# The last block's partial sums in another buffer, and the order of issue read from a table

## The chip, the cores and the metric

The kernel is written in Bass with Tile for a Trainium2 chip and runs on one of its cores. A core has five engines that run side by side, each through its own list of instructions in order: TensorE (PE: matrix products into PSUM), VectorE (DVE) and ScalarE (ACT: elementwise work), GpSimd (POOL) and SyncE (SP), which here issues every DMA. Where one engine needs what another makes, its instruction waits for a semaphore, and everything behind it in that engine's list waits with it.

The metric is the device time of one execution in microseconds, the median of several runs.

## The reference

q, k, v and g_ln are float32, the weight matrices 64-bit floats. The reference runs three stages, and each feeds the next:

```
B, H, S, D = 4, 8, 576, 64
scores = q @ k.T / sqrt(D)                       # per batch and head
mask   = local (rel in 0..31)  for heads 0..3,  strided (pos % 32 equal, rel >= 0)  for heads 4..7
x      = softmax(mask(scores)) @ v               # x: 2304 tokens x 512
h      = x @ w_in                                # 512 -> 1024
solu   = h * softmax(h);  ln = (solu - mean) / sqrt(var + 1e-6) * g_ln
y      = ln @ w_out                              # 1024 -> 512
out    = ((y @ w_a) * (y @ w_b)) @ w_out2        # 512 -> 1536 -> 512
```

The kernel reads each weight as a pair of 32-bit words and converts it itself.

## The kernel before

**Stages.** The attention runs batch by batch; scores, softmax and the product with V are made in tiles of a pair of heads. The strided heads use one form of mask, the local heads another. For batch 0's strided and local heads the probabilities are transposed on TensorE (L820) and multiplied with V in float32 (L854). For the other batches they are split into a high and a low half in float16 (`P2`), transposed by a DMA (`dma_start_transpose`, L842), and multiplied in three passes (L859 to L861), after a scale for V has been found by a chain of small steps (`pow2_scale`: TensorE L555, VectorE, TensorE L560, VectorE, TensorE L570). ScalarE copies the result to `xT` (L881). Tokens that are done go through the first feed-forward stage in tiles of 128 (`moe1`): x is split in two halves, L912 makes 1024 columns in three passes of 4 matmuls for each half, VectorE, ScalarE and GpSimd make softmax and normalisation, a DMA transposes the result, and `s2` multiplies by `w_out` (L966) and stores y to DRAM. All 2304 tokens pass before the last stage begins.

The last stage works on three blocks of 768 tokens (`SB`, `NSB`) and, for each, in three passes over thirds of the 1536 columns (`NP`, `UP`): nine blocks `b0` in all. The products of a block (L1392) follow a scheme with seven in place of eight products, for which y is split into sums and halves (`y_load`, L1306 to L1360). For passes 1 and 2 the last product (`out_pair`) follows the same scheme: seven products of six matmuls each per pair of token tiles, in two PSUM banks called M and N (L1530), with results updated by VectorE (L1546). For pass 0 it is `out_tile` (L1499).

**Partial sums.** A pass ends with 256 KB per token tile. Passes 0 and 1 store it to `o_scr` in DRAM; passes 1 and 2 load what the pass before has stored into a tile `ob` (L1517), add to it in place (L1546), and store it: to `o_scr` again, or to the output (L1568; in the very last pair column half by column half, L1573). There are two `ob` buffers of 128 x 2 x 512 numbers, used in turn, one for a pair. A block has three pairs.

**Weights.** Each 512 KB of raw weights comes in by `from_f64`: a DMA into one of three `raw64` buffers (L506, L509), a conversion on ScalarE (L510), a shift on VectorE (L516) and a merge on VectorE (L520). For `w_in`, ScalarE then rounds to a first half (L529) and GpSimd makes the rest (L530). `early` converts part of the last stage's weights during the attention and stores them to `w_scr` in DRAM, from where `conv_ab` reads them. A tile `yst` (128 x 4 x 768 float32) first holds y blocks while `y_load` splits them, and later the raw output weights of a pass (`conv_o`, `split_o`).

**What sets the order.** The program does not issue instructions as it goes. `P.op` notes an operation with its engine, its cost in the planner's eyes, what it reads and writes, and a function that emits it; operations are numbered as they are noted (3132 of them, 0 to 3131). At the end `Plan.schedule` puts them in one list, and `emit` calls them in that order, so that each engine gets its own operations in the order of the list. A dependency between engines becomes a semaphore wait. In the kernel before, `schedule` first follows due times (`P.key`), and then makes 200 further attempts: a backward pass gives each operation a key, noise is added, a forward pass lays the operations out with the planner's costs, and the order with the shortest result is kept.

Of the kernel before, what the change touches and what calls it, by code (L numbers as in the profile page):

```python
# [61 lines left out]


# [34 lines left out]
class Plan:  # L98

    TICK, ENTRY, SWITCH = 10.24 / 3, 2710, 0.095
    SAME = dict(DVE=0.13, ACT=0.15, POOL=0.05, PE=0.0, CTL=0.0)
    ENGINES = ("ACT", "CTL", "DVE", "PE", "POOL", "SP")

# [37 lines left out]
    def latency(self, a, b):  # L143
        if a.eng == b.eng and a.eng != "SP":
            return self.SAME[a.eng]
        return 0.28 if a.eng == "PE" else 0.14

    def schedule(self):


        ops, n = self.ops, len(self.ops)
        self.eng = [self.ENGINES.index(o.eng) for o in ops]
        self.us, self.cols, self.mode = [o.us for o in ops], [o.nbytes for o in ops], [o.mode for o in ops]
        self.deps = [[(d.seq, self.latency(d, o)) for d in sorted(o.deps, key=lambda d: d.seq)] for o in ops]
        self.starts = [[d.seq for d in sorted(o.starts, key=lambda d: d.seq)] for o in ops]
        self.outs, self.souts = [[] for _ in ops], [[] for _ in ops]
        for i in range(n):
            for d, lat in self.deps[i]:
                self.outs[d].append((i, lat))
            for d in self.starts[i]:  # L160
                self.souts[d].append(i)
        key, shift = [o.key for o in ops], 0.0
        order = self.forward(key, shift)
        self.mean = self.length(order)
        best = order, key, shift
        rnd = random.Random(PARAM["seed"])
        for t in range(PARAM["passes"]):
            if t % PARAM["back"] == 0 and t >= PARAM["first"]:
                self.forward(best[1], best[2])
            key = [k + rnd.gauss(0.0, PARAM["noise"]) for k in self.backward()]  # L170
            shift = self.TICK * (t % 4) / 4
            order = self.forward(key, shift)
            length = self.length(order)
            if length < self.mean:
                self.mean, best = length, (order, key, shift)
        return [ops[i] for i in best[0]]

    def length(self, order):
        return sum(self.replay(order, self.TICK * (k + 0.5) / 3) for k in range(3)) / 3

    def matmuls(self, count, t, us, cols):

        tick, per = self.TICK, cols / us if us else 0.0
        while True:
            w = int(t / tick)
            rate = 1.0 if w and count[w - 1] >= self.ENTRY else 0.5
            room = (w + 1) * tick - t
            if us <= room * rate:
                count[w] += per * us
                return t + us / rate  # L190
            count[w] += per * room * rate
            us -= room * rate
            t = (w + 1) * tick + 1e-9

    def replay(self, order, shift):
        eng, us, cols, deps, starts, mode, PE, SP = self.eng, self.us, self.cols, self.deps, self.starts, self.mode, 3, 5
        free, start, end = [0.0] * 6, [0.0] * len(eng), [0.0] * len(eng)
        count, dma, hw, was = [0.0] * 1000, 0.0, 0.0, 0
        for i in order:
            e = eng[i]  # L200
            at = free[e]
            for d, lat in deps[i]:
                x = end[d] + lat
                if x > at:
                    at = x
            for d in starts[i]:
                if start[d] > at:
                    at = start[d]
            start[i] = at
            if e == PE:  # L210
                x = us[i] if mode[i] == was else us[i] + self.SWITCH
                was = mode[i]
                end[i] = free[e] = self.matmuls(count, at + shift, x, cols[i]) - shift
            elif e == SP:
                hw = max(hw, at) + 0.55
                dma = max(dma, hw + 0.65) + cols[i] / 250e3
                free[e] = max(at + us[i], hw, dma - 2.0)
                end[i] = dma + 0.75
            else:
                end[i] = free[e] = at + us[i]  # L220
        return max(end)

    def forward(self, key, shift):
        eng, us, cols, outs, souts, mode, PE, SP = self.eng, self.us, self.cols, self.outs, self.souts, self.mode, 3, 5
        n = len(eng)
        left = [len(self.deps[i]) + len(self.starts[i]) for i in range(n)]
        ready, start, end = [0.0] * n, [0.0] * n, [0.0] * n
        free, coming, able = [0.0] * 6, [[] for _ in range(6)], [[] for _ in range(7)]
        push, pop = heapq.heappush, heapq.heappop
        for i in range(n):  # L230
            if not left[i]:
                push(coming[eng[i]], (0.0, i))
# [1451 lines left out]
```

## Time and profile before

| what | us |
|---|---|
| median of 3 runs | 705.09 |
| lowest and highest run | 704.83 and 705.89 |
| the profiled execution's own time | 706.01 |
| its span, first to last instruction | 704.2 |
| TensorE busy (95% of the span) | 671.1 |
| VectorE busy (79%) | 557.6 |
| ScalarE busy (61%) | 429.2 |
| GpSimd busy (21%) | 145.2 |
| mean granted clock of TensorE | 0.975 |

The profile is of one execution, which took 0.9 us more than the median. An engine is busy while it executes; waiting, branching and issuing DMAs don't count. Lines (L1530) are those of the kernel before. A row of the order of time gives start, duration, engine, line, operation and, in brackets, how long the engine had stood idle before and what ended that. `x3` means that three such instructions are drawn together. Matmuls overlap, since they are pipelined; their ends are modelled. The granted clock is a share of full speed: 1.00 is 2.4 GHz, 0.50 is 1.2 GHz.

### The profile page before, as it was taken

How to read it: one execution, taken by the hardware profiler on the slowest of the kernel's cores; microseconds unless marked ns; L12 is line 12 of the kernel's file. 1: busy time of each engine (PE TensorE's matmuls, PEld its weight loads, DVE VectorE, ACT ScalarE, POOL GpSimd, SP SyncE). 2: the span in 40 equal slices, each digit the busy share in tenths (PEclk: the TensorE clock that was granted, in tenths of full speed). 3: DMA queues.
4: the chain of work that ended last, by engine and by line, in shares of the span. 5: the costliest groups of instructions: out<-in, count | busy, mean ns of one | idle time of the engine just before them, and what ended most of it. 6: DMA issues, size and time to landing. Idle time of an engine off the chain costs nothing.

```text
span 704.2 us, 15205 instructions
## 1 busy us (share of the span) xinstructions
PE 671.1 (95%) x5861; PEld 483.9 (69%) x5861; DVE 557.6 (79%) x1189; ACT 429.2 (61%) x842; POOL 145.2 (21%) x268
## 2 busy tenths in 40 slices
PE   6877889999999999999899999999999999999996
PEld 5655668887888888886555555556767676776675
DVE  5878978967989654998999947779898978886584
ACT  3759757676877754867767537676545635534430
POOL 4544525633675442410000000000000000000000
PEclk9968789999999999999999999999999999999998
DMA  8978979889999834766462041672435206441035
GB/s 181 244 216 210 158 193 204 192 179 233 217 211 251 227 82 97 202 202 219 137 226 86 16 165 37 201 233 83 130 106 180 91 1 190 147 135 46 1 121 180
DMA packets 152645, 109.68 MB, mean 156 GB/s; under 512 B 103670, under 2 KB 128764, under 8 KB 152572
## 3 DMA queue, kind: packets, MB, share of 16 engines
q1 hardware_dynamic: 152572, 108.71, 58.5%
q8 instruction: 46, 0.75, 0.4%
q14 instruction: 27, 0.22, 0.1%
HBM read 65.42 MB, written 27.53 MB: 132 GB/s over the span
## 4 chain that ended last, share of the span: by engine, by line
PE 85%; DVE 5%; DMA 4%; ACT 2%; issue 1%; SPq 1%; POOL 0%; DVEq 0%; POOLq 0%; ACTq 0%
PE N L1392 19%; PE M L1392 14%; PE h L912 13%; PE y L966 13%; PE M L1499 6%; PE N L1530 6%; PE M L1530 5%; PE s L664 2%; DMA raw<-in_moe_w_a_dram 1%; PE s L757 1%; PE xbank L859 1%; DMA raw<-in_moe_w_b_dram 1%; DMA rawq<-in_q_dram 1%; DMA raw<-in_moe_w_in_dram 1%; DVE f64f L520 1%
## 5 line engine op out<-in xcount | busy, mean ns | idle before, releaser
L1392 PEld LDWEIGHTS <-w 128*128 128x128 f16 x1512 | 147.9, 98 | 95.3 <-issue 1.3
L1392 PE MATMUL N<-y,w 128*128 128x384 f16 x864 | 155.5, 326 | 0.0
L1392 PE MATMUL M<-y,w 128*128 128x384 f16 x648 | 119.2, 326 | 0.9 <-DVE y L1335 0.9
L966 PE MATMUL y<-lnT,wout 128*128 128x256 f16 x864 | 102.8, 275 | 2.1 <-ACT wout L579 2.1
L966 PEld LDWEIGHTS <-wout 128*128 128x128 f16 x864 | 82.5, 98 | 15.3 <-ACT wout L579 2.4
L912 PE MATMUL h<-win,xh 128*128 128x512 f32 x288 | 80.7, 423 | 2.4 <-DVE wk L927 2.4
L1530 PEld LDWEIGHTS <-p 128*128 128x128 f16 x693 | 67.7, 98 | 15.6 <-issue 3.5
L912 PEld LDWEIGHTS h<-win,xh 128*128 128x128 f32 x288 | 55.8, 201 | 14.5 <-DVE wk L927 2.6
L1484 ACT CAST p<-A 128x384 f16<-128x384 f32 x101 | 50.5, 512 | 22.1 <-DVE A L1459 19.6
L1489 DVE TENSOR_TENSOR p<-A,p 128x384 f16<-128x384 f32 x101 | 54.6, 552 | 6.6 <-ACT p L1484 6.4
L1530 PE MATMUL N<-wo,p 128*128 128x256 f16 x396 | 51.4, 273 | 3.1 <-DVE ob L1546 3.1
L1499 PE MATMUL M<-wo,p 128*128 128x512 f16 x216 | 49.9, 379 | 1.0 <-DVE A L1459 0.6
L510 ACT ACTIVATE f64f<-raw 128x512 f32<-128x512 f32 x52 | 34.6, 671 | 13.2 <-DMA raw<-in_moe_w_a_dram 4.9
L912 PE MATMUL h<-win,xl 128*128 128x512 f32 x144 | 40.1, 401 | 0.0
L1530 PE MATMUL M<-wo,p 128*128 128x256 f16 x297 | 38.6, 273 | 0.0
L1499 PEld LDWEIGHTS <-p 128*128 128x128 f16 x216 | 21.1, 98 | 24.6 <-issue 1.5
L833 POOL TENSOR_TENSOR e<-e,r 128x324 f32<-128x324 f32 (+2 forms) x30 | 27.2, 913 | 46.9 <-DVE r L794 43.2
L917 DVE TENSOR_REDUCE st<-h 128x1 f32<-128x1024 f32 x18 | 22.0, 1220 | 17.6 <-PE h L912 17.4
L1546 DVE SCALAR_TENSOR_TENSOR ob<-N,osc,ob 128x256 f32<-128x256 f32 x54 | 24.3, 477 | 14.3 <-PE N L1530 10.1
L1399 ACT COPY N<-N 128x384 f32<-128x384 f32 x36 | 16.6, 465 | 30.1 <-PE N L1392 29.5
L912 PEld LDWEIGHTS h<-win,xl 128*128 128x128 f32 x144 | 27.4, 194 | 6.4 <-issue 0.2
L841 POOL TENSOR_TENSOR P<-e,P 128x324 f16<-128x324 f32 (+2 forms) x30 | 28.4, 954 | 11.3 <-ACT P L840 11.2
(194 smaller groups left out, 1242.1 us busy)
## 6 DMA issues: line engine op xcount, KB each, us to landing
raw<-in_moe_w_out_dram SPq DMA_DIRECT2D x20, 512.0 KB
o_scr<-ob SPq DMA_DIRECT2D x36, 256.0 KB
ob<-o_scr SPq DMA_DIRECT2D x36, 256.0 KB
raw<-in_moe_w_a_dram SPq DMA_DIRECT2D x12, 512.0 KB
raw<-in_moe_w_b_dram SPq DMA_DIRECT2D x12, 512.0 KB
y_scr<-y SPq DMA_DIRECT2D x14, 384.0 KB
y<-y_scr SPq DMA_DIRECT2D x14, 384.0 KB
y_scr<-ys SPq DMA_DIRECT2D x18, 256.0 KB
```

What stands on the lines that cost most here:

```text
L510: act(0.67, lambda: nc.scalar.activation(f(), raw()[:, :, 1].bitcast(F32), AF.Prelu, scale=2.0 ** -112, alpha=-2.0 ** 32), (raw,), (f,))
L833: pool(0.1 + 1.2 * pl, lambda: nc.gpsimd.tensor_tensor(ev(), ev(), r()[:, :ng].unsqueeze(2).to_broadcast([128, ng, nk]), op=ALU.mult), (r, ...
L841: pool(0.15 + 1.4 * pl, lambda: nc.gpsimd.tensor_tensor(plo, ev(), ph, op=ALU.subtract), (e, ("P2", pi, 0)), (("P2", pi, 1),))
L912: nc.tensor.matmul(h()[:, 512 * n:512 * n + 512], xs[xa]()[:, kk], win[wa][:, kk, 512 * n:512 * n + 512], start=(pi == 0 and kk == 0), sto ...
L917: dve(1.22, lambda: nc.vector.tensor_reduce(st()[:, 0:1], h(), axis=AX.X, op=ALU.max, negate=True), (h,), ((st, 0),))
L966: nc.tensor.matmul(y()[:, 256 * mi:256 * mi + 256], wout[:, kk, wa, 128 * m:128 * m + 128], lnT()[:, xa, kk], start=(pi == 0 and kk == 0), ...
L1392: nc.tensor.matmul(to()[:, :HB], w()[:, wa, a, kk], y7[b]()[:, xa, kk], start=first and pi == 0 and kk == 0, stop=pi == 2 and kk == 1, ski ...
L1484: act(0.5, lambda: nc.scalar.copy(pu(0, a), x()), (x,), (pu.tok(0, a),))
L1489: dve(TD, lambda: nc.vector.tensor_tensor(pu(1, a), x(), pu(0, a), op=ALU.subtract), (x, pu.tok(0, a)), (pu.tok(1, a),))
L1499: nc.tensor.matmul(o(), pus[u](xa, 2 * t + c)[:, 128 * w:128 * w + 128], wo_whole(ps, 2 * u + c)[:, wa], start=(u == 0 and c == 0 and pi = ...
L1530: nc.tensor.matmul(bk(i), pus[u](xa, a)[:, 128 * tt:128 * tt + 128], wo()[:, u, b, wa], start=a == A11 and u == 0 and pi == 0, stop=u == U ...
L1546: dve(0.475, lambda: nc.vector.scalar_tensor_tensor(dst(), bk(i), s(), dst(), op0=ALU.mult, op1=ALU.add), (src, osc), ((ob, t, c),))
```

## The change

There are two parts.

First, in the last of the nine blocks `out_block` takes one more turn of the tile `yst` and hands it to `out_pair` as `spare`. The three pairs then use three separate parts of it (3 x 1024 of its 3072 columns), and no `ob`. Loads, updates and stores are as many and as large as before.

Second, the planner's passes are gone, and `schedule` returns the operations in the order of a list of their numbers, `ISSUE`. The operations and their numbers are the same as before. What an operation emits is unchanged, except for the buffer above. The numbers that the text below speaks of, with their place among their engine's operations in the order of before and in the table:

| number | what | engine, line | place before | in the table |
|---|---|---|---|---|
| 181 | load of the first block of `w_in` | SP L509 | 15 | 6 |
| 182 | its conversion | ACT L510 | 7 | 3 |
| 183, 184 | its shift and its merge | DVE L516, L520 | 28, 30 | 18, 25 |
| 190 | the merge of the second block | DVE L520 | 40 | 39 |
| 830, 853, 865 | products with V of batch 2's strided heads | PE L859 to L861 | 175, 180, 184 | 153, 157, 171 |
| 790, 792, 795 | a scale chain | PE L555, L560, L570 | 118, 145, 151 | 167, 170, 175 |
| 1084 | conversion of a block of `w_b` | ACT L510 | 191 | 199 |
| 1703 | first split of y for the second block | DVE L1335 | 484 | 479 |
| 1601, 1604, 1636 | halves of the first block's products | DVE L1489 | 470, 472, 478 | 493, 494, 497 |
| 1630, 1633 | sums of the first block's products | DVE L1403 | 480, 482 | 485, 487 |
| 1777 | an output product of the first block | PE L1499 | 401 | 403 |
| 3073, 3074, 3092, 3093, 3111, 3112 | loads of the last block's partial sums | SP L1517 | 384, 383, 389 to 392 | 365 to 370 |
| 3104 | last product of the last pair but one | PE L1530 | 792 | 790 |
| 3119, 3120 | products of the last pair | PE L1530 | 789, 791 | 791, 792 |
| 3123 | its last product | PE L1530 | 793 | 793 |

Of TensorE's 793 operations 292 keep their place, and the largest move is 49 places; of VectorE's 1024 it is 243, of ScalarE's 760 201, of GpSimd's 154 77, of SyncE's 398 138.

The diff, with the table and the passes taken out cut to a few lines:

```diff
+ISSUE = [int(n) for n in """
+5 0 13 2 14 1 11 15 10 12 29 6 16 8 35 181 9 4 3 37 7 36 414 430 771 787 39 38 43 40 41 182 66 44 17 55 42 45 67 56 20
+46 183 68 70 57 47 58 71 69 48 59 49 60 50 184 74 18 19 61 185 72 186 73 51 75 86 97 187 52 76 87 77 62 98 78 99 63 22
...
+883 1124 666 890 756 884 1123 830 889 1126 678 642 401 668 831 1125 667 643 1127 644 1130 891 669 674 1132 853 1070
+914 903 893 1143 1084 717 1144 694 904 923 1090 718 915 924 1145 905 719 1078 925 1085 935 1080 916 1146 886 720 948
...
+1634 1657 1606 1688 1938 1629 1607 1618 1603 1689 1692 1625 1693 1952 1620 1619 1690 1635 1627 1694 1691 1621 1628
+1698 1702 1695 1704 1631 1703 1659 1699 1675 1661 1696 1730 1723 1697 1744 1700 1732 1705 1706 1708 1734 1724 1711
...
+2808 2751 2773 2809 2740 2752 2748 2828 2753 2749 2768 2769 2747 2772 2810 2770 2706 2774 2829 2754 3073 2778 2750
...
+3081 3088 3099 3071 3082 3098 3083 3100 3084 3086 3101 3087 3085 3107 3090 3116 3102 3103 3117 3118 3089 3104 3106
+3091 3105 3119 3109 3126 3120 3108 3129 3121 3110 3122 3124 3123 3125 3130 3127 3128 3131
+""".split()]
...
-    def latency(self, a, b):
-        if a.eng == b.eng and a.eng != "SP":
-            return self.SAME[a.eng]
-        return 0.28 if a.eng == "PE" else 0.14
-
     def schedule(self):
...
-    def length(self, order):
-        return sum(self.replay(order, self.TICK * (k + 0.5) / 3) for k in range(3)) / 3
...
+        assert sorted(ISSUE) == list(range(len(self.ops)))
+        return [self.ops[i] for i in ISSUE]
...
-    def out_pair(ps, n, pus, tt, osc, cut):
-        Y, X, ob = bank("M"), bank("N"), rings["ob"].new()
+    def out_pair(ps, n, pus, tt, osc, cut, spare=None):
+        Y, X, ob = bank("M"), bank("N"), spare or rings["ob"].new()
+
+        def obv(i):
+            if spare:
+                return ob().rearrange("p k n -> p (k n)")[:, 2 * DM * tt + DM * i:2 * DM * tt + DM * i + DM]
+            return ob()[:, i]
+
+        def obt(i, c):
+            return ob, tt if spare else 0, i, c
         wo, H, gs = WO[ps], DM // 2, [SB // 128 * n + tt + 3 * i for i in range(2)]
         if ps:
             for i, g in enumerate(gs):
-                dma(lambda i=i, g=g: nc.sync.dma_start(out=ob()[:, i], in_=o_scr[ps - 1, g]), (("os", ps - 1, g),),
-                    ((ob, i, 0), (ob, i, 1)), 262144)
+                dma(lambda i=i, g=g: nc.sync.dma_start(out=obv(i), in_=o_scr[ps - 1, g]), (("os", ps - 1, g),),
+                    (obt(i, 0), obt(i, 1)), 262144)
 
         def bk(i):
             t = (X if i in (2, 3) else Y)()
@@ -1538,15 +1487,15 @@
             act(0.35, lambda: nc.scalar.copy(bk(j), bk(i)), (Y if i == 1 else X,), (X,))
 
         def add(i, t, c, old):
-            dst, src = (lambda: ob()[:, t, H * c:H * c + H]), (X if i in (2, 3) else Y)
+            dst, src = (lambda: obv(t)[:, H * c:H * c + H]), (X if i in (2, 3) else Y)
 
             def s():
                 return osc()[:, tt + 3 * t:tt + 3 * t + 1]
             if old:
                 dve(0.475, lambda: nc.vector.scalar_tensor_tensor(dst(), bk(i), s(), dst(), op0=ALU.mult, op1=ALU.add),
-                    (src, osc), ((ob, t, c),))
+                    (src, osc), (obt(t, c),))
             else:
-                act(0.47, lambda: nc.scalar.activation(dst(), bk(i), AF.Copy, scale=s()), (src, osc), ((ob, t, c),))
+                act(0.47, lambda: nc.scalar.activation(dst(), bk(i), AF.Copy, scale=s()), (src, osc), (obt(t, c),))
         mult(1, A11, B11)
         mult(4, S1, T1)
         again(1, 2)
@@ -1565,12 +1514,12 @@
         for i, g in enumerate(gs):
             to = out[128 * g:128 * g + 128, :] if ps == NP - 1 else o_scr[ps, g]
             if not cut:
-                dma(lambda i=i, to=to: nc.sync.dma_start(out=to, in_=ob()[:, i]), ((ob, i, 0), (ob, i, 1)), (("os", ps, g),),
+                dma(lambda i=i, to=to: nc.sync.dma_start(out=to, in_=obv(i)), (obt(i, 0), obt(i, 1)), (("os", ps, g),),
                     262144)
                 continue
             for c in (1, 0):
                 w = slice(H * c, H * c + H)
-                dma(lambda i=i, to=to, w=w: nc.sync.dma_start(out=to[:, w], in_=ob()[:, i, w]), ((ob, i, c),),
+                dma(lambda i=i, to=to, w=w: nc.sync.dma_start(out=to[:, w], in_=obv(i)[:, w]), (obt(i, c),),
                     (("os", ps, g, c),), 131072)
 
     ring("w2b", "V", [128, HB], F32, 2, c_b)
@@ -1598,10 +1547,12 @@
         P.key = at(b0) + UP * TU - 3
         dve(0.2, lambda: nc.vector.tensor_scalar(osc(), YSC[n](), ksc[:, ps, 1:2], None, op0=ALU.mult),
             (YSC[n], ("ksc", ps)), (osc,))
+        last = b0 == NP * NSB - 1
+        spare = rings["yst"].new() if last else None
         for tt in range(SB // 256):
             P.key = at(b0) + UP * TU + tt * TO
             if ps in pm["so"]:
-                out_pair(ps, n, pus, tt, osc, b0 == NP * NSB - 1 and tt == SB // 256 - 1)
+                out_pair(ps, n, pus, tt, osc, last and tt == SB // 256 - 1, spare)
             else:
                 ob = rings["ob"].new()
                 for k in range(2):
```

## Rows read from the trace of the kernel before

**Rows 1.** Busy by stretch: window, us; PE, PEld, DVE, ACT, POOL (count); clock, DMA share, GB/s.

```profile
0.00:103.00 103.00, 79.72 (x934) 62.25 (x935) 79.79 (x180) 68.36 (x133) 46.23 (x82) 0.85 0.86 201
27.00:43.00 16.00, 9.60 (x170) 7.47 (x162) 15.40 (x34) 11.62 (x25) 10.39 (x10) 0.74 0.77 206
44.00:103.00 59.00, 49.76 (x520) 38.31 (x519) 47.54 (x102) 43.29 (x84) 21.91 (x37) 0.82 0.85 194
103.00:338.00 235.00, 233.70 (x2552) 189.24 (x2551) 186.88 (x370) 166.94 (x306) 98.95 (x186) 1.00 0.84 196
338.00:352.00 14.00, 12.13 (x70) 6.67 (x69) 13.58 (x26) 10.20 (x18) 0.00 (x0) 1.00 0.26 82
352.00:691.00 339.00, 339.00 (x2256) 220.58 (x2255) 271.90 (x602) 183.35 (x386) 0.00 (x0) 1.00 0.35 115
```

**Rows 2.** The chain of waits from 690 us to the end: start, us, what.

```profile
691.71 3.06 DMA out_dram<-ob
...
694.84 3.44 DMA ob<-o_scr
```

**Rows 3.** Order of time from 691 us to the end, TensorE, VectorE and SyncE.

```profile
697.19 0.49 PE L1530 MATMUL N<-wo,p 128*128 128x256 f16 x3 [1.44 <-DVE ob L1546]
...
698.80 1.26 DVE L1546 SCALAR_TENSOR_TENSOR ob<-N,osc,ob 128x256 f32<-128x256 f32 x3
698.91 0.34 SPq L1573 DMA_DIRECT2D out_dram<-ob  x1
699.72 0.49 PE L1530 MATMUL N<-wo,p 128*128 128x256 f16 x3 [1.71 <-DVE ob L1546]
...
700.75 0.47 DVE L1546 SCALAR_TENSOR_TENSOR ob<-N,osc,ob 128x256 f32<-128x256 f32 x1
```

**Rows 4.** Order of time of SyncE's DMA issues from 595 to 622 us.

```profile
600.57 2.93 SPq L1375 DMA_DIRECT2D y<-y_scr  x3
617.59 4.38 SPq L1568 DMA_DIRECT2D out_dram<-ob  x4
```

**Rows 5.** TensorE's waits from 103 to 690 us: total us, times, longest us.

```profile
PE xbank L859 <- ACT xT L881: 1.1, 2, 0.6
PE M L1392 <- DVE y L1335: 0.9, 2, 0.5
PE M L1499 <- DVE A L1459: 0.6, 1, 0.6
```

**Rows 6.** Order of time of ScalarE from 160 to 182 us.

```profile
171.78 0.66 ACT L510 ACTIVATE f64f<-raw 128x512 f32<-128x512 f32 x1 [2.48 <-DMA raw<-in_moe_w_b_dram]
```

**Rows 7.** Order of time of VectorE from 8 to 24 us, and of ScalarE at 15.6.

```profile
11.43 0.89 DVE L788 TENSOR_REDUCE sm<-e 128x6 f32<-128x324 f32 x2 [0.45 <-ACT e L787]
14.49 0.90 DVE L775 TENSOR_REDUCE mx<-s 128x6 f32<-128x324 f32 x2 [1.75 <-PE s L757]
16.11 0.42 DVE L516 TENSOR_SCALAR raw<-raw 128x512 int32<-128x512 int32 x1
17.44 0.68 DVE L520 SCALAR_TENSOR_TENSOR f64f<-f64f,raw 128x512 int32<-128x512 int32 x1
23.16 0.55 DVE L788 TENSOR_REDUCE sm<-e 128x4 f32<-128x384 f32 x1 [0.93 <-ACT e L787]
...
15.60 0.66 ACT L510 ACTIVATE f64f<-raw 128x512 f32<-128x512 f32 x1 [2.60 <-DMA raw<-in_moe_w_in_dram]
```

**Rows 8.** Order of time of VectorE and GpSimd from 30 to 43 us.

```profile
30.66 1.28 POOL L530 TENSOR_TENSOR win<-f64f,win 128x512 fp32r<-128x512 f32 x1 [2.16 <-ACT win L529]
30.78 1.18 DVE L792 SCALAR_TENSOR_TENSOR sm<-sm,over 128x4 f32<-128x4 f32 x1
32.46 0.16 DVE L792 SCALAR_TENSOR_TENSOR sm<-sm,over 128x4 f32<-128x4 f32 x1
```

**Rows 9.** Order of time of SyncE's DMA issues from 159.8 to 172 us.

```profile
160.33 3.99 SPq L952 DMA_TRANSPOSE lnT<-ln  x1
```

More of the change, by code (lines that the diff above doesn't have):

```diff
@@ L1 @@
-import heapq
-import random
 from contextlib import ExitStack
@@ L98 @@
 class Plan:
-    TICK, ENTRY, SWITCH = 10.24 / 3, 2710, 0.095
-    SAME = dict(DVE=0.13, ACT=0.15, POOL=0.05, PE=0.0, CTL=0.0)
-    ENGINES = ("ACT", "CTL", "DVE", "PE", "POOL", "SP")
     def __init__(self):
@@ L141, in op @@
         return o
-    def latency(self, a, b):
-        if a.eng == b.eng and a.eng != "SP":
-            return self.SAME[a.eng]
-        return 0.28 if a.eng == "PE" else 0.14
     def schedule(self):
[L151 to L176, printed above, removed]
@@ L178, in length @@
-    def length(self, order):
-        return sum(self.replay(order, self.TICK * (k + 0.5) / 3) for k in range(3)) / 3
[L181 to L232, printed above, removed]
-        count, dma, hw, was, order = [0.0] * 1000, 0.0, 0.0, 0, []
-        for _ in range(n):
-            at = 1e9
-            for x in range(6):
-                t = free[x]
-                if not able[x] and not (x == PE and able[6]):
-                    if not coming[x]:
-                        continue
-                    t = max(t, coming[x][0][0])
-                if t < at:
-                    at, e = t, x
-            c = coming[e]
-            while c and c[0][0] <= at:
-                i = pop(c)[1]
-                push(able[6 if e == PE and mode[i] else e], (key[i], i))
-            a = able[e]
-            if e == PE and able[6]:
-                b = able[6]
-                if not a or b[0][0] + (0.0 if was else PARAM["stay"]) < a[0][0] + (PARAM["stay"] if was else 0.0):
-                    a = b
-            i = pop(a)[1]
-            start[i] = at
-            if e == PE:
-                x = us[i] if mode[i] == was else us[i] + self.SWITCH
-                was = mode[i]
-                stop = free[e] = self.matmuls(count, at + shift, x, cols[i]) - shift
-            elif e == SP:
-                hw = max(hw, at) + 0.55
-                dma = max(dma, hw + 0.65) + cols[i] / 250e3
-                free[e] = max(at + us[i], hw, dma - 2.0)
-                stop = dma + 0.75
-            else:
-                stop = free[e] = at + us[i]
-            end[i] = stop
-            order.append(i)
-            for d, lat in outs[i]:
-                if stop + lat > ready[d]:
-                    ready[d] = stop + lat
-                left[d] -= 1
-                if not left[d]:
-                    push(coming[eng[d]], (ready[d], d))
-            for d in souts[i]:
-                if at > ready[d]:
-                    ready[d] = at
-                left[d] -= 1
-                if not left[d]:
-                    push(coming[eng[d]], (ready[d], d))
-        self.start, self.end = start, end
-        return order
```

44 lines of the change are left out of this document (removed), and 117 rows, old and new, of the table ISSUE.

## The prediction

> **What bounds the kernel now.** Read busy time by stretch first, then TensorE's waits, then the chain of waits at the end, and last the order of time where those waits stand. TensorE is busy for 671.1 of the span's 704.2 us, and the stretches say where the other 33 lie [rows 1]. From 0 to 103 us it is busy for 79.72, at a mean granted clock of 0.85: the clock has two levels, 1.2 and 2.4 GHz, so 0.30 of the stretch, some 31 us, ran at 1.2. From 103 to 338 us only 1.3 us are free and from 352 to 691 none, all at full clock: there only fewer matmuls would help, and the change has as many. The rest is the step at 338 to 352 us (1.87 free) and the end. So what the change is worth comes from four places: the first 103 us, two waits near 175 us, the step at 338, and the end; and it can be lost in the 574 saturated us.
>
> **The end: the staging buffer.** In the last block each of three output pairs loads partial sums (L1517) into one of two `ob` buffers, and the third pair's loads wait until a buffer's results have been stored. The chain ends with the store of an older pair, 3.06 us, and the load that waits for it, 3.44 us [rows 2]. VectorE, and through it TensorE, stands still meanwhile: TensorE's last two groups of six write to banks that VectorE must read first, and wait 1.44 and 1.71 us [rows 3]. The change loads all six blocks into `yst`, idle since the last weights were split, at SP places 365 to 370. SyncE has cover there: the issues stand behind the last y reloads, of which three take 2.93 us and end at 603.5, and the next store leaves at 617.59 [rows 4]; six issues of no more than that take 6 of 14 us, and without that cover they would put off stores, not TensorE. So the load leaves the chain, and the sum goes on with what is late next. The table puts group 3104, which waited 1.44, ahead of the two groups before it, where its inputs are older: that wait goes. The last group still needs two updates of VectorE from the bank that the group before it fills: 0.84 (three take 1.26) and some 0.05 on either side to hand over, 0.94 in place of the 1.71 [rows 3]. What comes after the last group, an update and its store, stays. 1.44 + 1.71 - 0.94: **term -2.2.** Bounds: 0 if the two updates come late anyway, -3.15 if neither wait is left. That three pairs share a buffer adds no wait: a store left `ob` at 698.91, the store in the chain took 3.06 to land, and VectorE still wrote other columns of that `ob` at 700.75 [rows 2, 3].
>
> **The step at 338 us.** VectorE, busy for 13.58 of 14 us [rows 1], makes the next block's y operands here, and TensorE waits 0.9 for them (L1335) and 0.6 for L1459 [rows 5]. The table puts five updates of the older block (1601, 1604, 1636, 1630, 1633) behind the split 1703, which waited for them. One takes at least the 0.42 that a narrower one takes in [rows 3]: 2.1 us earlier, more than the 0.9. The group that waited 0.6 goes two groups back, 2 us of matmuls. What is left of the 1.87, under 0.4, I leave in. **Term: -1.5**, bounds 0 and -1.9. The updates put back must fit in later; from 352 on VectorE is busy 272 of 339 us [rows 1].
>
> **The waits near 175 us.** ScalarE stood 2.48 us at a weight conversion (L510) until its load landed [rows 6]; the bank evacuations behind it were late, and TensorE waited twice for them, 1.1 together [rows 5]. The table moves that conversion (1084) eight places back, behind instructions that were ready. **Term: -1.1**, bounds 0 and -1.1. Its result is late by as much; SyncE stores it to DRAM, and conv_ab reads it after the attention stage. Its raw buffer is free later too, which holds up weight loads, not attention's.
>
> **The first 103 us.** From 27 to 43 us VectorE is busy 15.40 of 16 [rows 1], and the first MoE matmul needs its last weight conversion and softmax, so what it does before 27 us counts. It waited 0.45, 1.75 and 0.93 there [rows 7]. The first weight load (181) goes from SP place 15 to 6. Its conversions 183 (0.42) and 184 (0.68) go ahead of the instructions that ended the first two waits or stood right behind them, and the second block's, 190, as long as 184, ahead of the third: 1.78 us of work move into waiting. ScalarE waited 2.60 for that load, until 15.60 [rows 7]; nine places sooner it must land some 5 us sooner, since ScalarE's conversion 182 now stands third, ahead of a bank evacuation. If it is later, transposes, scores and VectorE behind ScalarE lose what it is late. **Term: -1.8.** After 44 us the table shifts neighbours by five places or so, and I read no sum out of it. TensorE is free for 9.2 of those 59 us [rows 1]; so the bounds are -11 (all of it gone too) and +2.0 (rival C). I take the part that can be followed.
>
> **New waits.** On TensorE 501 of 793 operations change place. In 574 saturated us the order of before left 1.3 us; another order should leave as much at places of its own: **+1.3**, bounds 0 and +8 (rival D).
>
> **Sum.** -2.2 - 1.5 - 1.1 - 1.8 + 1.3 = -5.3. The profiled execution took 706.01 us (the span of 704.2 and 1.8 around it), so 700.7; the median of 705.09 is 0.9 below that execution: **699.8 us**. This case's own range is 697.5 to 702.2.
>
> **A rule to weigh.** From 30.78 to 31.96 a VectorE instruction on four numbers a partition took 1.18 us, where the next of its line takes 0.16, and ended with a GpSimd instruction that ran from 30.66 to 31.94 [rows 8]. The Trainium skill (SBUF — State Buffer, section "SBUF: two separate sides") says that VectorE and GpSimd share a pair of ports as an exclusive lock: whichever starts first holds it for its whole instruction, and the other is blocked. The trace agrees, with 1.18 against 0.16. By this rule an order that packs VectorE tighter beside the same GpSimd work can lose what it packs away, and the sum would be rival C's; without it the stretch keeps its 1.8.
>
> **Rivals.**
> A. *The table gives and takes alike; only the end holds.* For it: the saturated stretches have nothing to give, and a move that ends one wait can start another. Against it: the moves at 338 and 175 us answer to waits that stand in the rows. 705.09 - 2.2 = 702.9.
> B. *The first stretch closes up.* Half of the 9.2 us after 44 us goes too: 699.8 - 4.6 = 695.2. For it: the granted clock is 0.82 there [rows 1], low where TensorE had paused; fewer pauses may give clock back on top. Against it: VectorE is busy for 47.54 of the 59 us, ScalarE for 43.29, and they wait for each other.
> C. *VectorE is stretched beside GpSimd.* Single instructions are 1.0 too long [rows 8]; two more of them in place of the gain give +2.0 instead of -1.8: 703.6. For it: the same GpSimd work in less time. Against it: the conversions move to where there is less of it.
> D. *Slower: TensorE is stopped by products put in front.* Between 145 and 180 us three attention products (830, 853, 865) go 13 to 23 places ahead, in front of MoE matmuls. Their operand comes through transposing loads on SyncE, and one transpose held that queue 3.99 us [rows 9]; a product whose transpose stands behind such a one stops TensorE and all behind it. Two such stops cost 8.0: 707.8. It decides once new waits between 103 and 338 us are 5.3 above the forecast's. Against it: the transposes may be issued sooner too.
> E. *The load is out of the chain, but another wait takes its place*, so the end stays: 699.8 + 2.2 = 702.0. Against it: the rows name no other cause of the 3.15.
>
> **Chances.** Forecast 0.53, A 0.20, B 0.12, C 0.06, D 0.06, E 0.03. A measurement of this kernel can tell about 0.2%, 1.4 us, from no change, so faster means below 703.7. Faster: the forecast, B, three quarters of A, E, half of C: 0.86. Same: the rest of A and C: 0.08. Slower: D, 0.06. The range 694.8 to 703.9 leaves out D, the lower half of B, and the ends of the others, 2 in 10.
>
> **What would show it.** At the end: no wait of VectorE for `ob<-o_scr`, and one wait of TensorE of about 1.0 on L1530 in place of two. At 338 us: no wait on L1335. Near 175 us: ScalarE not waiting at L510, L859 without waits. Early: ScalarE's first L510 before 10.4, and the first matmul of L912 at about 43 us, where it was near 45. The prediction is wrong if TensorE's waits from 103 to 691 us exceed 5 us, if the first L912 starts no earlier, or if the span shrinks by more than 9.

## The result, and the profile after

The changed kernel takes **695.48 us** (median of 4 runs, 693.47 to 696.61) against 705.3 before: a ratio of 0.9857, 95% interval 0.9829 to 0.9885. The forecast was 699.8, its wide range 694.8 to 703.9, its own range 697.5 to 702.2; the direction was right and the gain is nearly twice as large, 9.8 us instead of 5.3.

Two cautions on these numbers. The profiled execution took 693.47, the fastest of the four, and the one before 706.01, so the pair of profiles shows 12.5 us. And both kernels scatter more than their first runs showed: 53 later runs of the kernel before lay between 702.8 and 710.3 (medians 705.4, 705.4 and 704.9 in three sets), nine runs of the changed one between 693.5 and 698.7, median 696.5.

Line numbers below are those of the changed kernel: up to the products of the last stage they are 59 lower than before (L912 is L853, L792 is L733, L530 is L471, L510 is L451, L1335 is L1276), in the output pairs 51 lower (L1530 is L1479, L1546 is L1495).

Busy time by stretch, columns as in [rows 1]; the later stretches are cut some 9 us sooner, where the same work now stands:

```profile
27.00:43.00 16.00, 12.48 (x192) 9.90 (x185) 14.91 (x35) 12.67 (x29) 11.13 (x11) 0.72 0.92 239
44.00:103.00 59.00, 51.96 (x636) 40.40 (x636) 51.27 (x105) 45.26 (x86) 24.46 (x43) 0.91 0.92 209
0.00:103.00 103.00, 84.58 (x1071) 67.28 (x1072) 84.52 (x187) 72.74 (x140) 50.31 (x88) 0.90 0.93 215
103.00:329.00 226.00, 225.32 (x2414) 181.31 (x2413) 177.43 (x361) 162.73 (x298) 92.82 (x181) 1.00 0.84 198
329.00:343.00 14.00, 12.85 (x78) 7.48 (x77) 13.75 (x26) 10.20 (x19) 0.00 (x0) 1.00 0.27 90
343.00:680.00 337.00, 337.00 (x2239) 218.80 (x2238) 271.32 (x600) 184.12 (x387) 0.00 (x0) 1.00 0.35 118
```

Read against [rows 1]: in the first 103 us TensorE does 1071 matmuls where it did 934, VectorE's busy time rises from 79.79 to 84.52, and the granted clock from 0.85 to 0.90. The saturated stretches look as before. TensorE's waits from 94 to 690 us (total, times, longest) are these, in place of [rows 5]:

```profile
PE N L1333 <- DVE C L1344: 0.9, 1, 0.9
PE y L907 <- DMA lnT<-ln: 0.7, 1, 0.7
PE M L1333 <- DVE y L1276: 0.2, 1, 0.2
```

1.8 us in place of 3.2: the waits near 175 us are gone, a new one of 0.68 stands at 115 us, and at 338 us 1.15 of 1.87 is left. The end, in order of time, VectorE and TensorE, answers to [rows 2, 3]:

```profile
686.71 0.88 DVE L1495 SCALAR_TENSOR_TENSOR yst<-N,osc,yst 128x256 f32<-128x256 f32 x2 [0.83 <-PE N L1479]
...
688.49 0.48 DVE L1495 SCALAR_TENSOR_TENSOR yst<-N,osc,yst 128x256 f32<-128x256 f32 x1
```

```profile
687.64 0.49 PE L1479 MATMUL N<-wo,p 128*128 128x256 f16 x3 [0.97 <-DVE yst L1495]
```

No load stands in the chain any more, VectorE waits for none, and TensorE's two waits of 1.44 and 1.71 have become one of 0.97.

Term by term, in the pair of profiles:

| place | forecast | measured |
|---|---|---|
| the end | -2.2 | waits 3.15 to 0.97: -2.2 |
| the step at 338 us | -1.5 | waits 1.87 to 1.15: -0.7 |
| near 175 us | -1.1 | waits 1.1 to 0: -1.1 |
| new waits, 103 to 338 us | +1.3 | a 0.68 in place of a 0.2: +0.5 |
| the first 103 us | -1.8 | the rest of 12.5: -9.0 |

By the medians the last row is smaller: 9.8 less the 3.5 of the others is 6.3, and over nine runs (705.3 to 696.5) 5.3. Either way it is about three times what was forecast or more, and all of the miss. The -9.0 holds scatter: a second profile of the changed kernel (e1, below) is 3.5 us later behind this stretch.

### The profile page after: what moved, and what is told of

The parts are those of the page before. It is cut to its first block, busy times and chain, and to the rows that moved or that the text cites. A ratio compares the mean times of both kernels' runs of the same rounds, so it can differ in the third digit from the quotient of the medians.

```text
span 691.7 us, 15210 instructions
## 1 busy us (share of the span) xinstructions
PE 667.2 (96%) x5861; PEld 481.2 (70%) x5861; DVE 554.1 (80%) x1189; ACT 430.1 (62%) x842; POOL 143.1 (21%) x268
## 4 chain that ended last, share of the span: by engine, by line
PE 87%; DVE 5%; DMA 3%; ACT 1%; issue 1%; SPq 1%; POOL 1%; DVEq 0%; POOLq 0%
PE N L1333 20%; PE M L1333 15%; PE y L907 14%; PE h L853 13%; PE N L1479 7%; PE M L1440 7%; PE M L1479 5%; PE s L605 2%; DMA rawq<-in_q_dram 1%; DMA raw<-in_moe_w_in_dram 1%; PE s L698 1%; PE xbank L800 1%; DMA lnT<-ln 1%; PE xbank L801 1%; PE xbank L802 1%
## 5 line engine op out<-in xcount | busy, mean ns | idle before, releaser
L907 PE MATMUL y<-lnT,wout 128*128 128x256 f16 x864 | 100.9, 273 | 0.7 <-DMA lnT<-ln 0.7
L853 PE MATMUL h<-win,xh 128*128 128x512 f32 x288 | 79.6, 418 | 2.2 <-DVE wk L868 1.6
L1479 PEld LDWEIGHTS <-p 128*128 128x128 f16 x693 | 67.8, 98 | 13.4 <-issue 1.1
L853 PEld LDWEIGHTS h<-win,xh 128*128 128x128 f32 x288 | 54.7, 198 | 13.7 <-DVE wk L868 1.6
L1479 PE MATMUL N<-wo,p 128*128 128x256 f16 x396 | 51.0, 273 | 1.0 <-DVE yst L1495 1.0
L451 ACT ACTIVATE f64f<-raw 128x512 f32<-128x512 f32 x52 | 35.1, 676 | 13.3 <-DMA raw<-in_moe_w_in_dram 4.4
L853 PE MATMUL h<-win,xl 128*128 128x512 f32 x144 | 40.7, 405 | 0.0
L1479 PE MATMUL M<-wo,p 128*128 128x256 f16 x297 | 38.3, 273 | 0.0
L873 DVE SCALAR_TENSOR_TENSOR ln<-wk,st,ln 128x1024 f16<-128x1024 f32 x18 | 23.5, 1304 | 10.2 <-ACT ln L872 10.2
L1340 ACT COPY N<-M 128x384 f32<-128x384 f32 x36 | 16.8, 467 | 23.7 <-PE M L1333 19.3
L853 PEld LDWEIGHTS h<-win,xl 128*128 128x128 f32 x144 | 27.3, 195 | 5.9
L774 POOL TENSOR_TENSOR e<-e,r 128x324 f32<-128x324 f32 (+2 forms) x30 | 24.4, 820 | 29.5 <-DVE r L735 21.0
L1355 ACT COPY V<-M 128x384 f32<-128x384 f32 x36 | 16.9, 479 | 21.5 <-PE M L1333 20.3
```

The costliest lines, as they stand in the source:

```text
L451: act(0.67, lambda: nc.scalar.activation(f(), raw()[:, :, 1].bitcast(F32), AF.Prelu, scale=2.0 ** -112, alpha=-2.0 ** 32), (raw,), (f,))
L774: pool(0.1 + 1.2 * pl, lambda: nc.gpsimd.tensor_tensor(ev(), ev(), r()[:, :ng].unsqueeze(2).to_broadcast([128, ng, nk]), op=ALU.mult), (r, ...
L853: nc.tensor.matmul(h()[:, 512 * n:512 * n + 512], xs[xa]()[:, kk], win[wa][:, kk, 512 * n:512 * n + 512], start=(pi == 0 and kk == 0), sto ...
L873: dve(1.3, lambda: nc.vector.scalar_tensor_tensor(ln()[:, 1], e(), st()[:, 3:4], ln()[:, 0], op0=ALU.add, op1=ALU.subtract), (e, (st, 3), ...
L907: nc.tensor.matmul(y()[:, 256 * mi:256 * mi + 256], wout[:, kk, wa, 128 * m:128 * m + 128], lnT()[:, xa, kk], start=(pi == 0 and kk == 0), ...
L1355: act(TA, lambda: nc.scalar.copy(t4(), b4()[:, :HB]), (b4,), (t4,))
```

## The experiments

"New" is the order of the table, "old" the order of the kernel before. Every kernel has its order written out as a table; the diffs show how it was made. Changes of time are against runs of the kernel before on the same chip: e1 to e4 ran on one, e5 to e8 on a second, e9 to e12 on a third.

**Where the gain stands (four kernels).** One is the changed kernel unchanged; the others change order at a cut.

```diff
-        return [self.ops[i] for i in ISSUE]
+        a, b = NEW, OLD            # e3_first44_old: a, b = OLD, NEW, with the spare buffer
+        head = a[:a.index(296) + 1]  # e4_first103_new: 345
+        return [self.ops[i] for i in head + [i for i in b if i not in head]]
```

> The changed kernel once more, as the partner of the next three. Its four runs so far lay in two pairs, 693.5 and 694.5 at a mean granted clock of 0.985 and 0.984, and 696.5 and 696.6 at 0.979 and 0.980. If the clock of the first stretch makes the pairs, new runs fall into the same two groups, each with its clock; if it is scatter of something else, the times fill the space between and don't go with the clock.

> The table's order up to the first matmul of the MoE stage (33 operations of TensorE, 79 of VectorE, 49 of ScalarE, 21 of GpSimd, 41 of SyncE, the same ones in both orders), the old order and the old staging buffers from there. Theory early: the moves before 44 us carry the first stretch; the first L912 starts 3.4 us sooner, the pauses after it close because their inputs come sooner, and at 103 us the kernel is 7 to 9 us ahead: 696 to 698. Rival late: the later pauses are closed by the moves that stand there; only the 3.4 are passed on: 701 to 702. The forecast's term for these moves was 1.8: 703.

> The complement: the old order up to the first matmul of the MoE stage, the table and the spare buffer from there. Theory early: nothing is gained by 103 us, and 0.6 near 115 to 175 us, 0.7 at 338 and 2.2 at the end remain: about 701.5. Rival late: some 5 us are gained between 44 and 103 us, on top of these 3.5: about 696.5.

> The table's order up to the last second-layer product before 103 us, the old order and the old staging buffers from there. If the four places add up as the two profiles say, it is 8.8 us below the kernel before, 696 to 697, with the waits of 1.1 near 175 us, 1.87 at 338 and 3.15 at the end as before. If the order behind the cut must fit the order ahead of it, new waits come right behind 103 us and the gain is smaller.

(The heads of e2 and e3 hold the same operations but for two of each.) Measured: e1 696.92 (5 runs, 694.45 to 698.69), -8.5; e2 701.50 (8 runs), -3.9, ratio 0.9941 (0.9917 to 0.9966); e3 698.33 (6 runs), -7.1, ratio 0.9899 (0.9870 to 0.9928); e4 701.29 (6 runs), -4.2.

The idea of two groups of runs falls: e1's fastest run had the lowest clock of its five, 0.979. Of the two theories neither holds alone. The new order up to 44 us is worth 3.9 by itself. The rest is worth 7.1, of which the terms behind 103 us are 3.5; so some 3.6 would come from 44 to 103 us, a difference and not a kernel of its own. The two do not add up: together they are 7.5, and the whole order gives 5.0 in e1 and 6.3 in the first runs. The profiles say the same. The last stage's first product has the same 348 operations of TensorE ahead of it in every kernel, and starts so in the kernel before, the changed kernel, e1, e2 and e3:

```profile
303.31 0.98 PE L1392 MATMUL M<-y,w 128*128 128x384 f16 x5
294.52 0.65 PE L1333 MATMUL M<-y,w 128*128 128x384 f16 x3
298.05 1.14 PE L1333 MATMUL M<-y,w 128*128 128x384 f16 x6
297.47 0.81 PE L1333 MATMUL M<-y,w 128*128 128x384 f16 x4
297.80 0.49 PE L1333 MATMUL M<-y,w 128*128 128x384 f16 x2
```

With the new order only up to 44 us, or only behind it, or throughout, the three kernels stand 5.3 to 5.8 ahead: in these profiles either part alone gives what both give. The second and third row are of one kernel, so a single profile is good to some 3.5 us here, and how far the parts overlap is not measured more closely. The first matmul of L853, at 44.83 in the kernel before, starts at 40.89 in e2 and at 44.87 in e3:

```profile
40.89 2.06 PE L853 MATMUL h<-win,xh 128*128 128x512 f32 x4
```

```profile
44.87 1.65 PE L853 MATMUL h<-win,xh 128*128 128x512 f32 x3
```

In e4, with the new order up to 103 us, the gain is 0.3 more than e2's, and the cut cost something, as its rival said. TensorE's waits from 45 to 690 us in e4 have two behind the cut, at 107 and 208 us:

```profile
PE xbank L800 <- DMA PT<-P: 2.0, 2, 1.7
PE xbank L501 <- ACT xT L822: 1.0, 1, 1.0
```

**The forecast's own step for the first 103 us.** Only the five operations that it named and the two halves that follow from them (185 on ScalarE, 186 on GpSimd) change place.

```diff
+        for i in (181, 182, 183, 184, 185, 186, 190):   # each behind its neighbour in NEW
+            order.insert(order.index(neighbour(i)) + 1, order.pop(order.index(i)))
```

> The kernel before with the seven operations of the forecast's step for the first 103 us at the table's places: the load 181, the conversion 182, shift and merge 183 and 184, the two halves 185 and 186, and the second block's merge 190. Forecast: the first L912 starts 1.8 us sooner, near 43.0, and the time falls by 1.8 to 2. Rival, these seven carry all of it: 41.5, as in the changed kernel, and 3.4 or more. Rival, the chain that ends at the first L912 is another: 44.8 as before, no change.

Measured: 705.16 (10 runs), ratio 0.9992 (0.9974 to 1.0011): no change. The first L853 starts 0.8 sooner:

```profile
44.05 2.50 PE L853 MATMUL h<-win,xh 128*128 128x512 f32 x5
```

So the part "that can be followed" was not what the table gains by.

**What VectorE loses to GpSimd.** Up to its last step ahead of the first L853 VectorE has the same 79 operations in every kernel. For each I took what it ran longer than in the profile where it ran shortest, and added that up: 5.5 us in the kernel before, 3.7 in the changed one. In the six kernels with the old order up to there it is 5.3 to 5.7, in the seven with the new one 3.6 to 4.0; VectorE's last step ends at 44.14 and 41.64, and of these 2.5 us 1.8 are this and 0.7 less idle time. The steps that ran too long lie beside instructions of GpSimd, most of them the subtraction for the second halves of `w_in`. One from the kernel before (start, duration, what), which takes 0.15 by itself:

```profile
35.56 1.23 DVE L792 SCALAR_TENSOR_TENSOR sm<-sm,over 128x4 f32<-128x4 f32 x1
```

In the new order GpSimd does six of the eight subtractions in two packs of three:

```profile
25.62 4.38 POOL L471 TENSOR_TENSOR win<-f64f,win 128x512 fp32r<-128x512 f32 x3
...
36.71 3.73 POOL L471 TENSOR_TENSOR win<-f64f,win 128x512 fp32r<-128x512 f32 x3
```

and VectorE loses less beside them. Of its steps that lost more than 0.1 us, six stand beside a subtraction in the kernel before, with 4.8 us in all, and four in the changed one, with 2.2. The packing by itself was not tried. To see what the collisions themselves cost, the subtractions were left out of the kernel before:

```diff
+        nc.vector.memset(win[1].rearrange("p k n -> p (k n)").bitcast(F32), 0.0)   # once, at 6 us
+    for i in (186, 192, 198, 204, 210, 216, 222, 228):
+        P.ops[i].fn = lambda: None
```

> The kernel before without GpSimd's eight subtractions that make the second halves of w_in (the halves are zeros here, set once by VectorE at 5 us, where it stood idle for 3.9 us). Up to its last step ahead of the first L912 VectorE had 32.1 us of work, 4.4 on top by instructions that ran too long beside GpSimd, and 7.7 idle. Theory lock: the 4.4 fall under 1.5, VectorE's last step ends 3 us sooner or more, and the first L912 starts near 41.5. Rival: VectorE isn't what the first L912 waits for; what it no longer loses to GpSimd it stands idle, and the first L912 stays near 44.8.

Measured (one run): 702.99, profile: the sum falls to 0.8 (with the shortest times of all profiles, its own among them, it is 5.5 before, not 4.4). VectorE's last step ends at 42.28, 1.9 sooner and not 3, since it then waits for other things; the first L853 starts at 41.63. One group of one line shows it best, VectorE's steps of 128x4 in the first 103 us, with the busy time, the mean and the idle time before them; kernel before, changed kernel, and this one:

```profile
L792 DVE SCALAR_TENSOR_TENSOR sm<-sm,over 128x4 f32<-128x4 f32 x7 | 3.2, 457 | 0.0
```

```profile
L733 DVE SCALAR_TENSOR_TENSOR sm<-sm,over 128x4 f32<-128x4 f32 x7 | 1.8, 257 | 0.1
```

```profile
L733 DVE SCALAR_TENSOR_TENSOR sm<-sm,over 128x4 f32<-128x4 f32 x7 | 1.1, 156 | 0.0
```

The same seven steps on four numbers take 3.2, 1.8 and 1.1 us. The theory holds for the mechanism, with one thing beside it: e11 also makes GpSimd's own list shorter. TensorE's last wait ahead of the first L853 is for a product of GpSimd (L824, L765). In the kernel before, a subtraction stood in front of that product, and it started 1.05 us after VectorE's last input to it (41.40); in the changed kernel 0.90 after (39.50), in e11 0.05 after (38.66). The wait before, and the product in the three kernels:

```profile
43.19 0.66 PE L820 MATMUL y<-ident,e 128*96 128x128 f32 x2 [1.56 <-POOL e L824]
```

```profile
42.45 1.15 POOL L824 TENSOR_TENSOR e<-e,r 128x192 f32<-128x192 f32 x2
40.40 1.60 POOL L765 TENSOR_TENSOR e<-e,r 128x192 f32<-128x192 f32 x2
38.71 0.97 POOL L765 TENSOR_TENSOR e<-e,r 128x192 f32<-128x192 f32 x2 [2.24 <-DVE r L735]
```

So of the 3.7 us by which e11 starts it sooner 2.7 are VectorE's and 1.0 GpSimd's own; of the changed kernel's 2.1, 1.9 are VectorE's. The theory holds only in part for the time: this kernel had 3.2 us in hand at 42 us and one run 1.9 below the median of before, with the granted clock at 0.82 in the first 103 us. Waits as long as those of the kernel before stand behind it:

```profile
PE xbank L496 <- ACT xT L822: 2.5, 1, 2.5
PE s L693 <- ACT qkT L612: 2.1, 1, 2.1
```

The Trainium skill (SBUF — State Buffer, section "SBUF: two separate sides") says that the shared ports are locked for a whole instruction, not divided, and that only some of VectorE's instructions need them. The trace agrees: the step of 1.23 us reads four numbers a partition and loses 1.08, nearly the whole of a subtraction (1.27 to 1.53 us), while a reduction of VectorE beside the second pack (L716 at 37.02) takes its usual 0.36.

**What the clock costs.** Two kernels got transposes of a constant ahead of the operations that TensorE waited for; their results are not read.

```diff
+FILL = {129: 6, 165: 7, 315: 8, 270: 11, 539: 6, 332: 9}   # e8: 129: 5, 141: 6, 475: 9, 270: 5, 350: 3, 539: 1, 422: 2, 369: 8
         for o in order:
+            for _ in range(FILL.get(o.seq, 0)):
+                nc.tensor.transpose(unused_bank_columns(o), ident, ident)
             o.fn()
```

> The kernel before, its order and buffers untouched, with 47 extra transposes of a constant on TensorE, put right ahead of six operations that waited 1.45 to 2.49 us there; their results are never read. At 0.16 us each they take 7.5 of the 11 us of these pauses. Theory clock: the granted clock fell to half after these pauses, so with them filled the low time ahead of 103 us, 30.7 us in the profile, falls to 10 or less, and the time by 3 to 5 us, to about 701, with no pause closed. Rival: the low clock costs nothing there, since TensorE waits for others anyway: the low time falls but the time stays at 705. Rival: the extra work delays what stands behind it: slower.

> The changed kernel with 39 such extra transposes ahead of eight operations that waited 0.33 to 1.96 us. Theory clock: low time ahead of 103 us falls from 20 to under 10 us, and the time by 2 to 4, to about 693 by the median, below both kernels. Rivals as for the kernel before: no change, 696.5; or slower.

Measured: e7 704.54 (12 runs), ratio 0.9988 (0.9964 to 1.0011), no change; e8 694.15 (4 runs), 0.9836 (0.9814 to 0.9858), against e1's 0.9871 (0.9842 to 0.9899, on another chip), whose interval overlaps. The first 103 us, the first row e7, the second e8:

```profile
0.00:103.00 103.00, 83.67 (x999) 67.03 (x1000) 79.79 (x180) 67.98 (x133) 46.06 (x82) 0.92 0.85 200
```

```profile
0.00:103.00 103.00, 83.65 (x1080) 66.69 (x1081) 84.12 (x186) 71.15 (x138) 49.04 (x85) 0.93 0.93 210
```

The filling did raise the clock: in e7 from 0.85 to 0.92, 14 us less at 1.2 GHz and 17 left where 10 were expected; in e8 to 0.93. So the low clock follows from these pauses. In e7 one filling also cost time: the eleven transposes put ahead of the wait of 2.49 had to wait for VectorE themselves, and the product behind them started 1.3 us later than in the kernel before (the first of these rows).

```profile
69.26 0.37 PE L555 MATMUL xbank<-ident,wam 128*8 128x128 f32 x1 [2.49 <-ACT xT L881]
```

```profile
69.07 1.72 PE L1598 MATMUL s<-ident 128*128 128x128 f32 x11 [2.46 <-DVE e L725]
70.58 0.42 PE L496 MATMUL xbank<-ident,wam 128*8 128x128 f32 x1
```

The higher clock made that good: at 104 us e7 is 1.9 ahead of the kernel before (the same product for the scores at 104.07 and 106.01). But by the median the kernel before gains nothing by the filling; VectorE's busy time to 103 us is 79.79, what it was before, and TensorE stops again right behind, for a transposing load:

```profile
105.91 0.22 PE L800 MATMUL xbank<-PT,V 54*64 54x54 f16 x2 [1.43 <-DMA PT<-P]
```

The 3 to 5 us of the clock theory did not come in the kernel before: what the clock gives there, the next wait takes, less what the filling itself put off. Whether the clock is worth 2 us in the changed kernel is not settled here.

**The three places behind 103 us, by themselves.**

```diff
+        # old order, with: 1084, 1085, 1086 later (places 199, 276, 279);
+        # 1601, 1604, 1630, 1633, 1636 and 1777 at NEW's places; spare buffer, its six loads at SP 365 to 370
```

> The kernel before with three groups of moves and nothing else. Near 175 us: conversion 1084 eight places back on ScalarE, its shift and merge behind it. At 338 us: the updates 1601, 1604, 1630, 1633, 1636 of VectorE at the table's places, behind the split 1703, and the product 1777 two groups back. At the end: the six loads into the spare buffer at the table's places, 3104 where it was. By the forecast's steps TensorE's waits near 175 us go from 1.1 to 0, at 338 us from 1.87 to under 0.4, and at the end from 3.15 to some 1.9 (two handovers of 0.94, since 3104 stays behind). Rival for 338 us: update 1630 comes too late and stops TensorE by about 0.9, as in the changed kernel, so 1.1 or more stays.

Measured (one run, 709.09): near 175 us no wait is left, as forecast. At the end one wait of 0.43 is left of 3.15, less than with the whole table: the load's leaving removes 2.7 of it, and the table's order of the last groups brings 0.5 of waiting back (0.97).

```profile
702.79 0.49 PE L1479 MATMUL N<-wo,p 128*128 128x256 f16 x3 [0.43 <-DVE yst L1495]
```

At 338 us the rival was right, and more than it said:

```profile
346.79 2.08 PE L1333 MATMUL N<-y,w 128*128 128x384 f16 x6 [5.22 <-DVE C L1344]
```

Product 1632 reuses a bank that update 1630 must read first. With 1630 behind the split and 1632 where it was, TensorE stands 5.22 us, its clock is down to half for 6.8 us from inside that wait on, and the kernel, 1.2 us ahead until then, is 6 us late to the end. The table had also put 1632 three groups back, and so pays only 0.92 for it (update at 337.61, product at 338.22):

```profile
337.61 0.55 DVE L1344 TENSOR_TENSOR C<-N,V 128x384 f32<-128x384 f32 x1
```

```profile
338.22 1.14 PE L1333 MATMUL N<-y,w 128*128 128x384 f16 x6 [0.92 <-DVE C L1344]
```

**One long wait between 44 and 103 us.**

```diff
+        # old order, with 156, 178, 309 on ScalarE at places 66, 73, 74 and 311 on GpSimd at 26
```

> The kernel before with four operations of the stretch from 44 to 103 us at about the table's places: on ScalarE the bank evacuations 156 and 178 and the first tile's square 309, 13 to 15 places sooner, on GpSimd the step 311 that follows, 7 places sooner. Theory: 156 holds the bank that the first scale chain (L555) waits 2.49 us for, the longest pause there; with it gone 2.5 us are gained, and the low clock from 69 to 76 us goes too, 3 to 5 us in all: 701 to 702.5. Rival: ScalarE is as full, and the pause comes back at another place: 705.

Measured: 706.97 (12 runs), ratio 1.0026 (1.0006 to 1.0046): slower by a little. The pause is not gone, it has grown, and it ends with another operation of ScalarE (L488), which now stands behind the moved ones:

```profile
70.28 0.38 PE L496 MATMUL xbank<-ident,wam 128*8 128x128 f32 x1 [4.64 <-ACT f64f L488]
```

**Two places of the table mended.**

```diff
-... 1705 1708 1711 1630 ...
+... 1705 1630 1708 1711 ...
+        # operations 3075 to 3131 (without the loads) in the relative order of OLD
```

> The changed kernel with two places of the table mended: VectorE's update 1630 three places sooner, ahead of the sums 1708 and 1711, and the operations of the last three output pairs in the relative order of the kernel before (with 3104 behind 3119 and 3120). Expected: the stop of 0.92 at 338 us goes, 1.15 becomes 0.23; the last wait falls from 0.97 to 0.4, as with the buffer alone; 1.4 us in all, so 695 by the median of the table's nine runs, 696.5. Rival: VectorE is so full at 338 us that the wait only moves to what needs the sums 1708 and 1711: 1.15 stays.

> The kernel with the two mended places and, on top, the same 39 transposes of a constant in TensorE's pauses as before. The filled changed kernel took 694.15 against 696.5, at a clock of 0.990 against 0.982. Theory clock: 2 us or more below the mended kernel without them, near 692.5, in every place of its range. Rival, as the filled kernel before showed (704.5 against 705.4): the clock gives back under 1 us, 694 to 695.

Measured: e9 697.33 (4 runs), ratio 0.9888 (0.9871 to 0.9905); e10 695.97 (5 runs), 0.9862 (0.9842 to 0.9883). The wait for 1630 is gone and another has come, for a copy by ScalarE (L1361), so with the 0.22 on L1276 1.0 of the 1.15 stays; at the end waits of 0.43 and 0.2 are left. That is some 0.5 us, which a measurement can't see. The rival was right for 338 us in size, though the wait is not for what needs the two sums:

```profile
343.03 1.46 PE L1440 MATMUL M<-wo,p 128*128 128x512 f16 x6 [0.78 <-ACT A L1361]
```

Filled and not filled differ by 1.4 us here and by 2.8 between e8 and e1 (two chips), with the same sign and overlapping intervals. No kernel tried is shown to be faster than the changed one; e8 has the lowest median.

## Why the prediction was right, and where it was not

- **The number** was right by little, and partly by luck: 695.48 lies 0.7 inside the wide range and 2.0 below this case's own (697.5 to 702.2). The terms outside the first stretch add up to -3.5 as forecast, but only because two errors cancel: 0.8 lost at 338 us, 0.8 less of new waits. And a measurement was said to tell 0.2% from no change, where the scatter above leaves 0.3% either way.
- **The end** was right in cause and size: a wait of 0.97 was measured for a forecast of 0.94. One detail was not: putting 3104 ahead was credited with the 1.44 that went. By e5 the buffer alone does it, and leaves less waiting (0.43).
- **Near 175 us** was right: with 1084, its shift and its merge moved and the table's other moves there left out both waits went (e5). ScalarE still waits for a weight load there, 2.64 us at 160.7, but at a place where TensorE has other work.
- **The step at 338 us** was half right. "The updates put back must fit in later" was said and not followed: the term asked when VectorE's split would be ready, not which product reuses the bank that the put-back update 1630 reads. It measured -0.7 for -1.5.
- **New waits**: 0.68 at 115 us and the 0.92 at 338. With the two terms above, 103 to 691 us were forecast at -1.3 and measured at -1.4 (waits of 3.2 became 1.8). Rival D did not come, and the 5 us that would have refuted the forecast there were far off.
- **The first 103 us** is the step that failed: -1.8 was forecast, 5.3 to 9.0 were measured. Its working failed, not just its size. It credited the moves of the first two weight blocks with filling VectorE's waits; by themselves they move the first L853 by 0.8 and the time not at all (e6). One of its signs was wrong too: ScalarE's first L451 started at 11.11, not before 10.4, since the load took until then, and it held up what stood behind it:

```profile
11.11 0.68 ACT L451 ACTIVATE f64f<-raw 128x512 f32<-128x512 f32 x1 [3.07 <-DMA raw<-in_moe_w_in_dram]
```

  The other sign came out further than it said: the first L853 at 41.46, forecast 43. And "if the span shrinks by more than 9" was met, with 12.5 in the profiles. The prediction called that wrong, and for this stretch it is.
- **What stood in place of it.** Up to 44 us the whole order counts: 3.9 us by e2, and in the trace 2.5 us of VectorE's, most of them time that it lost to GpSimd. Rival C had this mechanism and the row for it [rows 8], and gave it the wrong sign: a reorder can also pull the collisions apart. But the rest of the order gives as much without it (3.6 by e3), and the two together hardly more than one. The prediction read "no sum out of it" behind 44 us, which was honest, but then took nothing as the value between bounds of +2 and -11. Rival B, half of that free time, came to 695.2 and was the best number in the text, with a chance of 0.12; its split, 1.8 ahead of 44 us and 4.6 behind, is borne out by no run.
- **What stays open**: which moves give the gain between 44 and 103 us, and why either part of the order by itself gives nearly what both give. The one pause singled out did not yield to its own four moves (e12), and TensorE's, VectorE's and ScalarE's orders were not tried one by one.

## What to carry to other kernels

In this kernel the searched order was worth most where several engines are nearly full and wait for each other, and least where TensorE is full: forecast the first by a share of its free time (half of it came nearest here), not by the moves that can be followed one at a time. And don't add up what parts of such an order give by themselves: here each half gave nearly the whole. A few moves taken out of it are no test either: one group cost 7 us at 338 us, because a product that the table puts back on another engine was left where it was, and another group cost 2. And before a step is put back on one engine, look for the bank or buffer that it frees, and who writes there next.

## What the runs showed of the hardware

What VectorE loses beside GpSimd was more than expected: 5.5 us in 44, nearly all of it gone when eight GpSimd instructions were left out (0.8), and one step on four numbers went from 0.15 to 1.23 us. In the new order, where six of GpSimd's eight subtractions stand back to back, the loss is 3.7. And 14 us more at 2.4 GHz in the first 103 us, 0.92 against 0.85, were worth 0.8 us with an interval that includes none: e7 was 1.9 us ahead at 104 us in the profile and stood 1.43 at the next wait.
